# A two-layer attention and feed-forward prompt kernel: the first tiles taken one by one, and every engine's order written out

## The chip, the cores and the metric

The kernel runs on one core of a Trainium2 chip. A core has five engines with instruction streams of their own: TensorE (PE in the profile; PEld is its weight loads), VectorE (DVE), ScalarE (ACT), GpSimd (POOL) and SyncE (SP, which here only starts DMA transfers). An engine runs its own instructions strictly in the order in which they stand, and waits on semaphores for the others. The metric is the device time of the one launch in microseconds, as a median of several runs.

## The reference

The input x has 2048 tokens of 640 features. Two layers follow, each an attention with a memory over segments and then a feed-forward part, both with the same weights in both layers.

```python
    x = A_x
    x = x + _A_ref(_layernorm(x, axis=-1), A_wq, A_wk, A_wv, A_wo, A_beta)
    x = x + _B_ref(_layernorm(x, axis=-1), B_w1, B_w2)
    x = x + _A_ref(_layernorm(x, axis=-1), A_wq, A_wk, A_wv, A_wo, A_beta)
    x = x + _B_ref(_layernorm(x, axis=-1), B_w1, B_w2)
```

`_A_ref` splits the tokens into 4 segments of 512, with 32 heads of 20 features. In a segment it computes causal softmax attention within the segment, and a second term that is read from a memory matrix M and a normaliser z, which all earlier segments have written:

```python
            logits = jnp.einsum('bhqd,bhkd->bhqk', qs, ks) * scale + mask
            p = _softmax(logits, axis=-1)
            a_dot = jnp.einsum('bhqk,bhkd->bhqd', p, vs)
            pq = phi(qs)
            num = jnp.einsum('bhld,bhde->bhle', pq, M)
            den = jnp.einsum('bhld,bhd->bhl', pq, z)[..., None] + 1e-06
            o = g * (num / den) + (1.0 - g) * a_dot
            pk = phi(ks)
            M = M + jnp.einsum('bhld,bhle->bhde', pk, vs)
            z = z + jnp.einsum('bhld->bhd', pk)
```

(`a_mem` is written out here.) `_B_ref` is `maximum(x @ w1, 0) @ w2` with 1728 hidden features.

## The kernel before

Tokens are handled in tiles of 128, four of which make a segment. All of x and all weights stay in SBUF. Per layer and segment the work is: layer norm of the four tiles, with a transpose, so that features lie on partitions (`xnT`); the projections to q and k (`proj_part`, evacuated from PSUM into `stg`) and to v (`proj_v`, into `v_aug`); a way through device memory that spreads the heads of q and k over partitions (`spill` writes `scr`, `fill` reads it into `pad`; for the first two groups of heads `first_heads` copies straight from `stg`); scores of four heads at once as 20-row matmuls (`scores`, into the PSUM pairs X and Y); their exponentials on ScalarE (`exps`, into `PT`); the causal cut on GpSimd; values as 32-column matmuls (`apply`) or, for two early groups, by token (`values_by_token`); the memory's reading and writing (`mem_read`, `mem_write`); the output projection, and then the feed-forward part (`ffn`, `ffn_last`). Full-array matmul groups take one of four PSUM banks, the list `MISC`, and each bank is evacuated by VectorE or ScalarE before its next use.

Nothing of the order is written by hand. Each piece of work is a Python generator, called a stream, which yields operations with an engine, an estimated duration and the results that it waits for. `Sched` holds 33 streams with priorities and goes on picking the operation that can start first by its own clock. It places each on an engine (an evacuation may go to VectorE or ScalarE), gives out slots (PSUM banks, staging buffers), and puts semaphore waits in front. Where its clock shows TensorE idle for over 0.3 us, `keep_busy` puts in matmuls of a unit matrix that nobody reads (L638; dummies from here on). `plan` is run 48 times, each with another cost for changing between full-array, row-tiled and column-tiled matmuls (`STARTS`, 79 to 114 ns), and the plan with the least time in `late`, a replay with random lateness of the loads, is emitted.

The head is written apart. `first_ln_a` takes tiles 0 and 1 and `first_ln_b` tiles 2 and 3. Tiles 0, 1 and 3 have their statistics from VectorE (`stats`), tile 2 from ScalarE by two passes with accumulation. Both hand over to `first_pair`, which normalises two tiles on VectorE, transposes each on TensorE by the unit matrix (five 128-column matmuls) and copies the result from PSUM to `xnT`. `proj_first` then projects in groups of 256 columns, tiles 0 and 1 together, then tiles 2 and 3:

```python
        order = [(c, n, h) for h in range(2) for c in range(2) for n in range(2)]
        order += [(c, n, h) for c in range(2, FC) for h in range(2) for n in range(2)]
        for c, n, h in order:
            tk = yield from proj_part(0, 0, c, n, h)
```

Here c is the chunk of 128 output features, n is 0 for k and 1 for q, and h is the pair of tiles. From tile 0's arrival on, TensorE runs 43 dummies of `warm_pe` (L634).

Of the kernel before, what the change touches and what calls it, by code (L numbers as in the profile page):

```python
# [6 lines left out]
dt = mybir.dt  # L7
# [153 lines left out]
STARTS = [SWITCH_NS + 0.75 * (k - 48 // 2) for k in range(48)]  # L161
# [14 lines left out]

class Sched:


    def __init__(self, prog, switch):  # L180
        self.P = prog
        self.switch = switch
        self.log = []
        self.free = {e: 800.0 for e in ENGS}
# [8 lines left out]
    def keep_busy(self, op, start):  # L193
# [10 lines left out]
        if n > 1:  # L204
            self.log.append(("pe", 56.0 * n, 0.0, s.tks, [], False))
            self.P.waits("pe", s.tks)
            for _ in range(n):
                self.P.op("pe", lambda e, ap=s.ap: self.idle_fn(e, ap), False)
# [62 lines left out]
    def run(self):  # L271
        while True:
# [84 lines left out]
            self.log.append((e, hold, tail, waits, out if isinstance(out, list) else [out], op.dma is not None))  # L357
            st[2], st[3] = None, ((slot, out) if slot is not None else out,)

# [59 lines left out]
def plan(switch, sb, sem_, psum, dram, A_x, A_wq, A_wk, A_wv, A_wo, A_beta, B_x, B_w1, B_w2, out):  # L419
# [248 lines left out]
    def chain(t0, n, tk, sq=None):  # L668
# [7 lines left out]
        tk = yield pool(760, lambda e: e.tensor_tensor(rstd[:, sl], lnU[:, sl], mhalf[:, 0:n], ALU.pow), [tk] + h)  # L676
# [43 lines left out]
    def first_pair(p, tch):  # L720
        idt = yield Need("ident")
        if p == 0:
            xt = yield Acq(XNT_A)
            xt.users = []
            S.set("xts", 0, 0, tks=[xt])
        else:
            xt = yield Need("xts", 0, 0)
            xt = xt[0]
        bx = yield Acq(XN)
        done = []  # L730
        tns = []
        for k in range(2):
            tn = yield normed(2 * p + k, k, bx, tch[k])
            tns.append(tn)
        for k in range(2):
            t = 2 * p + k
            tn = tns[k]
            pb = lambda bk: bk.ap.bitcast(dt.bfloat16)
            fns = [(lambda e, bk, c=c, k=k: e.transpose(
                pb(bk)[:, c * 128:(c + 1) * 128], bx.ap[:, k * D + c * 128:k * D + c * 128 + 128], ident[:]),  # L740
                c == FC - 1) for c in range(FC)]
            bk, tT = yield pe((88.0 if p == 0 else 56.0) * FC, fns, [tn] + idt, acq=MISC)
            dst = xt.ap[:, t * FC:(t + 1) * FC, :].rearrange("p c n -> p (c n)")
            src = pb(bk)[:, 0:D]
            tc = yield evac(D, 1.5, lambda e, dst=dst, src=src: e.tensor_copy(dst, src),
# [783 lines left out]
def bass_interleave_layers__memory_aug_infini_attn__dense_activation_relu__prompt_kernel(  # L1529
    nc, A_x, A_wq, A_wk, A_wv, A_wo, A_beta, B_x, B_w1, B_w2, out,  # L1530
):
    with contextlib.ExitStack() as es:
# [13 lines left out]
        with nc.Block() as block:  # L1546
            S.P.emit(block)
# [29 lines left out]
```

## Time and profile before

| | us |
|---|---|
| median of 3 runs | 562.49 (562.12 to 563.04) |
| the profiled execution | 562.46 |
| its span in the trace | 560.6 |
| TensorE busy | 555.5 |
| VectorE busy | 410.8 |
| ScalarE busy | 409.7 |
| GpSimd busy | 194.3 |

A row of the timeline gives the start and the duration in microseconds, the engine, the line of the kernel, the operation and its tiles (written<-read), the shapes, and how many consecutive instructions were merged. In brackets stands how long the engine idled ahead of it, and what ended that. A matmul's duration contains its way through the array, during which the next ones already run; how densely they follow is seen from the distance of their starts. In the table of DMA issues the last number is the median time from issue to landing.

### The profile page before, as it was taken

How to read it: one execution, taken by the hardware profiler on the slowest of the kernel's cores; microseconds unless marked ns; L12 is line 12 of the kernel's file. 1: busy time of each engine (PE TensorE's matmuls, PEld its weight loads, DVE VectorE, ACT ScalarE, POOL GpSimd, SP SyncE). 2: the span in 40 equal slices, each digit the busy share in tenths (PEclk: the TensorE clock that was granted, in tenths of full speed). 3: DMA queues.
4: the chain of work that ended last, by engine and by line, in shares of the span. 5: the costliest groups of instructions: out<-in, count | busy, mean ns of one | idle time of the engine just before them, and what ended most of it. 6: DMA issues, size and time to landing. Idle time of an engine off the chain costs nothing.

```text
span 560.6 us, 12651 instructions
## 1 busy us (share of the span) xinstructions
PE 555.5 (99%) x5110; PEld 302.6 (54%) x5111; DVE 410.8 (73%) x1060; ACT 409.7 (73%) x522; POOL 194.3 (35%) x302
## 2 busy tenths in 40 slices
PE   8999999999999999999999999999999999999998
PEld 7654545545644455645356554465445654665655
DVE  5898899776998787877888987889824866651202
ACT  5799999987699779787897789877856788323140
POOL 4534344333354444344433443335401433100000
DMA  8599988741374137443373505550325510422101
GB/s 269 118 201 219 254 202 164 172 123 44 90 175 99 50 89 185 88 99 79 97 179 52 127 20 137 131 120 20 67 77 154 114 43 20 93 69 55 41 1 47
DMA packets 132219, 61.43 MB, mean 110 GB/s; under 512 B 111042, under 2 KB 122050, under 8 KB 132162
## 3 DMA queue, kind: packets, MB, share of 16 engines
q1 hardware_dynamic: 131942, 60.37, 45.7%
q8 instruction: 40, 0.66, 0.5%
q10 hardware_dynamic: 220, 0.26, 0.2%
q14 instruction: 17, 0.14, 0.1%
HBM read 20.57 MB, written 12.85 MB: 60 GB/s over the span
## 4 chain that ended last, share of the span: by engine, by line
PE 90%; DVE 8%; DMA 1%; ACT 0%; POOL 0%; issue 0%
PE ps L654 58%; PE ps L651 12%; PE ps L1114 9%; PE ps L1257 7%; DVE stats L662 2%; PE ps L1058 2%; PE ps L1007 2%; DVE x_sb L1328 1%; PE ps L1405 1%; DVE stg L827 1%; DMA x_sb<-in_A_x_dram 1%; DVE xn_tok L704 1%; DVE av L1265 0%; DVE xn_tok L716 0%; DVE mv L664 0%; ACT PT L1166 0%
## 5 line engine op out<-in xcount | busy, mean ns | idle before, releaser
L1166 ACT ACTIVATE PT<-ps 128x1024 bf16<-128x1024 f32 x320 | 310.1, 1022 | 66.1 <-PE ps L1114 64.5
L1178 POOL TENSOR_SCALAR_AFFINE_SELECT PT<-PT 128x512 bf16<-128x512 bf16 x256 | 166.3, 668 | 267.7 <-ACT PT L1166 267.7
L654 PE MATMUL ps<-w_r,hT 128*128 128x320 bf16 (+2 forms) x768 | 123.4, 299 | 0.1
L654 PE MATMUL ps<-xnT,w_r 128*128 128x512 bf16 x416 | 113.6, 379 | 0.0
L1328 DVE TENSOR_TENSOR x_sb<-x_sb,ps 128x320 bf16<-128x320 bf16 (+1 forms) x128 | 60.4, 479 | 70.2 <-PE ps L654 69.9
L654 PEld LDWEIGHTS ps<-w_r,hT 128*128 128x128 bf16 x768 | 72.2, 98 | 34.2 <-issue 6.3
L1436 ACT ACTIVATE hT<-ps 128x512 bf16<-128x512 f32 x55 | 33.0, 599 | 46.4 <-PE ps L654 46.1
L1114 PE MATMUL ps<-pad 20*128 20x384 bf16 (+3 forms) x1024 | 64.9, 301 | 0.0
L654 PEld LDWEIGHTS ps<-xnT,w_r 128*128 128x128 bf16 x416 | 39.7, 98 | 42.1 <-issue 2.9
L662 DVE BATCH_NORM_STATS2 stats<-x_sb 128x6 f32<-128x320 bf16 x126 | 55.9, 470 | 2.3 <-DMA x_sb<-in_A_x_dram 2.0
L1265 DVE CAST av<-ps 128x512 bf16<-128x512 f32 x56 | 38.3, 684 | 12.9 <-PE ps L1257 12.5
L1114 PEld LDWEIGHTS ps<-pad 20*128 20x128 bf16 x1024 | 18.2, 92 | 51.4 <-ACT PT L1166 24.2
L654 PE MATMUL ps<-wo_r,oT 128*128 128x320 bf16 x256 | 45.3, 299 | 0.0
L1434 DVE TENSOR_SCALAR hT<-ps 128x512 bf16<-128x512 f32 x49 | 33.5, 684 | 10.5 <-PE ps L654 10.0
L1257 PE MATMUL ps<-PT,v_aug 128*32 128x256 bf16 (+5 forms) x896 | 40.7, 302 | 0.0
L651 PE MATMUL ps<-xnT,w_r 128*128 128x512 bf16 x104 | 39.6, 381 | 0.0
L654 PE MATMUL ps<-wv_r,xnT 128*128 128x320 bf16 x192 | 35.8, 300 | 0.0
L654 PE MATMUL ps<-xnT,wk_r 128*128 128x512 bf16 (+1 forms) x140 | 35.5, 349 | 0.0
L676 POOL TENSOR_TENSOR rstd<-lnU,mhalf 128x2 f32<-128x2 f32 (+2 forms) x25 | 20.3, 811 | 39.9 <-DVE lnU L672 39.7
L654 PE MATMUL ps<-xnT,wq_r 128*128 128x512 bf16 (+1 forms) x140 | 33.9, 349 | 0.0
L1301 DVE TENSOR_TENSOR o_sb<-avt,rden 128x320 bf16<-128x320 bf16 x60 | 33.3, 572 | 0.7
L654 PEld LDWEIGHTS ps<-wo_r,oT 128*128 128x128 bf16 x256 | 24.8, 98 | 11.3 <-issue 1.3
(120 smaller groups left out, 686.9 us busy)
## 6 DMA issues: line engine op xcount, KB each, us to landing
pad<-scr SPq DMA_DIRECT2D x124, 80.0 KB
scr<-stg SPq DMA_DIRECT2D x34, 256.0 KB, 2.9
out_dram<-x_sb SPq DMA_DIRECT2D x15, 160.0 KB, 1.8
w_r<-in_B_w_dram SPq DMA_DIRECT2D x10, 216.0 KB, 3.3
w_r<-in_B_w_dram SPq DMA_DIRECT2D x13, 160.0 KB, 2.7
x_sb<-in_A_x_dram SPq DMA_DIRECT2D x9, 160.0 KB, 3.3
scr<-w_r SPq DMA_DIRECT2D x5, 256.0 KB, 3.5
x_sb<-in_A_x_dram SPq DMA_DIRECT2D x3, 320.0 KB, 7.3
```

Source lines behind the costliest of these rows:

```text
L651: bk, tk = yield pe(mm_ns(n), [(lambda e, bk, a=a, b=b: e.matmul(bk.ap[:, 0:n] if len(b.shape) == 2 else bk.ap[:, 0:n].rearrange("p (i n) ...
L654: tk = yield pe(mm_ns(n), [(lambda e, k=k, a=a, b=b, bk=bk: e.matmul(bk.ap[:, 0:n] if len(b.shape) == 2 else bk.ap[:, 0:n].rearrange("p (i ...
L662: tk = yield dve(320, 1, lambda e, c2=c2: e.bn_stats(stats6[:, t, c2, :], x_sb[:, t, c2 * 320:(c2 + 1) * 320]), xt)
L1114: fns.append([(lambda e, z=z, j=j, hh=hh, N=N, o=o, sl=sl: e.matmul(ps[:, hh, o:o + N], sl.ap[32 * hh:32 * hh + DH, z, 0, 128 * j:128 * j ...
L1166: tx = yield act(1024, lambda e, dst=dst, src=src: e.activation(dst, src, ACT.Exp, scale=SCALE), sc + pw)
L1178: tm = yield pool(600.0, lambda e, reg=reg: e.affine_select(out=reg, in_=reg, pattern=[[0, 4], [1, 128]], compare_op=ALU.is_ge, fill=0.0, ...
L1257: fns.append((lambda e, bk, j=j, hh=hh, pt=pt, g=g0 + z: e.matmul(bk.ap[32 * hh:32 * hh + wide(g, hh), 128 * j:L], VAUG[vx(a, s)][:, j].re ...
L1265: te = yield evac(L, 1, lambda e, sl=sl, z=z, bk=bk: e.tensor_copy(sl.ap[:, z], bk.ap), lambda e, sl=sl, z=z, bk=bk: e.activation(sl.ap[:, ...
L1301: to = yield dve(320, 1, lambda e, dst=dst, src=src, rz=rz: e.tensor_tensor(dst, src, rz, ALU.mult), [tg] + OSB.tks)
L1328: ta = yield dve(n, 1, lambda e: e.tensor_tensor(x_sb[:, t, c0:c0 + n], x_sb[:, t, c0:c0 + n], bk.ap[:, 0:n], ALU.add), [tk] + list(waits) ...
L1434: th = yield evac(512, 1, lambda e, dc=dc, bk=bk: e.tensor_scalar(hT[:, dc, :], bk.ap[:, :], 0.0, None, ALU.max), lambda e, dc=dc, bk=bk: ...
L1436: lambda e, dc=dc, bk=bk: e.activation(hT[:, dc, :], bk.ap[:, :], ACT.Relu), [tk] + HT.tks)
```

## The change

Three things change.

First, the head goes by single tiles. `first_tile(t)` replaces the two layer norm streams and `first_pair`. Tiles 0 and 1 have their statistics from VectorE, tiles 2 and 3 from ScalarE. Each tile has its own power on GpSimd, its own normalisation, transposes and copy. A list `TURN` fixes VectorE's order among them. The transposes go to the PSUM pairs X and Y in place of `MISC`. `proj_tile` projects tile 0 and tile 1 with 128-column matmuls, each into its half of the same bank, for the first two chunks of k and q, and one evacuation takes both halves. What then remains goes in groups of 256 as before, with the k group of chunk 2 on tiles 0 and 1 drawn ahead.

Second, one plan is made in place of 48, with a change of mode at 79 ns.

Third, the plan's order is not emitted. `Sched` records each operation with its stream, and `in_turns` lines them up anew: `TURNS` holds a string for each engine, in which each letter names the stream whose next operation comes (a is the first stream added, and so on; dummies stand as J on TensorE). Within a stream, on one engine, the order stays; which engine does an operation and which slot it has also stay as planned. Semaphore waits are derived again for the new order. The strings have 322 letters for SP, 518 for ScalarE, 1065 for VectorE, 299 for GpSimd and 2904 for TensorE, and were found by a search that moved runs of operations.

Counted in the built programs, TensorE has 5138 matmuls in place of 5111: 40 of 128 columns for 20 of 256, and 104 dummies for 97 (the 43 of `warm_pe` among them).

```diff
-STARTS = [SWITCH_NS + 0.75 * (k - 48 // 2) for k in range(48)]
+STARTS = [79.0]
...
+TURNS = {
+    "sp": (
+        "HHHHHHHHGHlllllmlmyyllllsmIIIIllslmeImlllIIIlIylysmIIIemmlIIIImlllllIIIsllmmlIIlgglyymeIlIlllmmjkels"
...
+    "pe": (
+        "FJJuzzzzzzvzzzzzzwzzzzzzzzzzzzzzzzzzxzzzzzzzzzzzzzzzzzzzzzzzzzzzzzCCzCCzzzzzzCCCCCCzzzzzCCCCCCCCCCCC"
...
+    def in_turns(self, turns):
...
+        for e, order in turns.items():
+            assert sorted(order) == sorted(n for n, rs in todo[e].items() for _ in rs), e
+            its = {n: iter(rs) for n, rs in todo[e].items()}
+            seq[e] = [next(its[n]) for n in order]
+        P = Prog(self.P.clk)
...
+                    P.waits(e, [new[t] for t in waits])
...
+    TURN = ["s0", "s0", "a0", "s1", "l0", "s1", "n0", "m2", "a1", "l1", "m3", "c0", "n1", "l2", "c1"]
...
+    def first_tile(t):
+        p, k = divmod(t, 2)
+        w = yield Need(("x0a", "x0b", "x01", "x01")[t])
+        if p == 0:
+            for c2 in range(2):
+                tk = yield from in_turn("s%d" % t, dve(320, 1.1, lambda e, c2=c2: e.bn_stats(
+                    stats6[:, t, c2, :], x_sb[:, t, c2 * 320:(c2 + 1) * 320]), w))
...
+        else:
+            junk = hT[:, 10 - 3 * k:13 - 3 * k, :].rearrange("p c n -> p (c n)")[:, 0:D]
+            ta = yield act(D + 350, lambda e: e.activation(
+                junk, x_sb[:, t, :], ACT.Copy, accum_out=asum[:, t:t + 1]), w, psum=False)
...
+        tch = yield pool(560, lambda e: e.tensor_tensor(
+            rstd[:, t:t + 1], lnU[:, t:t + 1], mhalf[:, 0:1], ALU.pow), [tk] + h)
...
+        bk, tT = yield pe((88.0 if t == 0 else 56.0) * FC, fns, [tn] + idt, acq=[X, Y])
...
+    def proj_tile(t, n, c):
...
+        for k in range(FC):
+            mm = lambda e, bk, k=k: e.matmul(
+                bk.ap[:, 128 * t:128 * t + 128], w_r[:, k, c * 128:(c + 1) * 128],
+                xt.ap[:, t * FC + k, :], start=(k == 0), stop=(k == FC - 1))
...
+        te = yield evac(256, 1, lambda e: e.tensor_copy(sg.ap[:, 0:256], src),
+                        lambda e: e.activation(sg.ap[:, 0:256], src, ACT.Copy), [tk] + sg.tks)
...
     def proj_first():
-        order = [(c, n, h) for h in range(2) for c in range(2) for n in range(2)]
-        order += [(c, n, h) for c in range(2, FC) for h in range(2) for n in range(2)]
+        for t in range(2):
+            for n in range(2):
+                for c in range(2):
+                    yield from proj_tile(t, n, c)
+        order = [(2, 0, 0)] + [(c, n, 1) for c in range(2) for n in range(2)]
+        order += [x for x in [(c, n, h) for c in range(2, FC) for h in range(2) for n in range(2)] if x != (2, 0, 0)]
...
-    S.add(5, first_ln_a())
-    S.add(5, first_ln_b())
+    for t in range(4):
+        S.add(1 + 0.2 * t, first_tile(t))
...
-            S.P.emit(block)
+            S.in_turns(TURNS).emit(block)
```

More of the change, by code (lines that the diff above doesn't have):

```diff
@@ L725, in first_pair @@
             S.set("xts", 0, 0, tks=[xt])
-        else:
[L727 to L745, printed above, removed]
-                            lambda e, dst=dst, src=src: e.activation(dst, src, ACT.Copy), [tT])
-            bk.release(tc)
-            done.append(tc)
```

202 lines of the change are left out of this document (169 added, 33 removed).

## The prediction

> **What bounds the kernel now.** I read the page first (engine shares, then the chain that ended last), then TensorE's timeline for the spacing of its matmuls and for its gaps, then the three engines at the head, then the DMA issues.
>
> ```profile
> PE 555.5 (99%) x5110; PEld 302.6 (54%) x5111; DVE 410.8 (73%) x1060; ACT 409.7 (73%) x522; POOL 194.3 (35%) x302
> ...
> PE 90%; DVE 8%; DMA 1%; ACT 0%; POOL 0%; issue 0%
> ```
>
> TensorE is busy for 99% of the span and carries 90% of the chain. A busy share counts pipelined matmuls whole, so the test is the distance from one start to the next.
>
> ```profile
> 30.63 0.38 PE L654 MATMUL ps<-hT,wk_r 128*128 128x512 bf16 x1
> 30.84 0.30 PE L651 MATMUL ps<-wv_r,hT 128*128 128x320 bf16 x1
> 30.98 0.71 PE L654 MATMUL ps<-wv_r,hT 128*128 128x320 bf16 x4
> 31.52 0.38 PE L654 MATMUL ps<-hT,wk_r 128*128 128x512 bf16 x1
> 31.83 0.39 PE L1114 MATMUL ps<-pad 20*128 20x512 bf16 x4
> 32.16 0.31 PE L651 MATMUL ps<-wv_r,hT 128*128 128x320 bf16 x1
> ...
> 557.39 0.83 PE L654 MATMUL ps<-w_r,hT 128*128 128x128 bf16 x12
> 558.06 0.22 PE L654 MATMUL ps<-w_u,hL 128*128 128x128 bf16 x1
> ```
>
> A start-to-start distance is 0.21 us for 512 columns (30.63 to 30.84), 0.135 for 320 (four in 30.98 to 31.52) and 0.056 for 128 (twelve in 0.67 us). The row at 31.52 is another 512-column matmul, but the score matmuls behind it start 0.31 us later: leaving full-array work for 20-row scores costs 0.096 us. The score block takes 0.33 us until the next full-array matmul. TensorE is bound by its own columns, so only three things can shorten the run: an earlier start of real work, fewer mode changes or dummies, and fewer gaps. The large gaps are these:
>
> ```profile
> 79.47 0.62 PE L638 MATMUL ps<-ident 128*128 128x128 bf16 x8
> 80.36 0.34 PE L1007 MATMUL ps<-BD,w_r 128*128 128x84 bf16 x3 [0.27 <-DVE om_sb L1018]
> ...
> 99.87 0.34 PE L1007 MATMUL ps<-BD,w_r 128*128 128x147 bf16 x3
> 100.47 0.31 PE L651 MATMUL ps<-wv_r,xnT 128*128 128x320 bf16 x1 [0.25 <-DVE av L1265]
> ...
> 324.17 0.38 PE L654 MATMUL ps<-xnT,w_r 128*128 128x512 bf16 x1
> 324.64 0.29 PE L638 MATMUL ps<-ident 128*128 128x128 bf16 x2
> ```
>
> Eight dummies fill 0.45 us after 79.47, and 80.36 leaves a gap of 0.44. The memory read at 99.87 holds three matmuls of some 0.06 us each, and 100.47 leaves 0.42. After 324.17, 0.47 less 0.21 is 0.26. Together that is 1.12 us in 550.
>
> **The head.**
>
> ```profile
> 4.86 0.74 ACT L764 ACTIVATE hT<-x_sb 128x640 bf16<-128x640 bf16 x1 [2.11 <-DMA x_sb<-in_A_x_dram]
> 5.50 0.19 ACT L764 ACTIVATION_READ_ACCUMULATOR hT<-x_sb 128x1 f32 x1
> 5.99 0.83 ACT L768 ACTIVATE hT<-x_sb,mv 128x640 bf16<-128x640 bf16 x1 [0.30 <-DVE mv L766]
> ...
> 6.87 0.43 DVE L716 TENSOR_SCALAR xn_tok<-x_sb,mv,rstd 128x640 bf16<-128x640 bf16 x1
> ...
> 7.88 0.48 DVE L745 COPY xnT<-ps 128x640 bf16<-128x640 bf16 x1
> ...
> 6.15 1.05 PE L638 MATMUL ps<-ident 128*128 128x128 bf16 x10
> 7.36 0.45 PE L739 MATMUL ps<-ident,xn_tok 128*128 128x128 bf16 x5 [0.15 <-DVE xn_tok L716]
> ...
> 9.06 0.81 PE L739 MATMUL ps<-ident,xn_tok 128*128 128x128 bf16 x10 [0.19 <-DVE xn_tok L716]
> 9.71 0.27 PE L651 MATMUL ps<-xnT,wk_r 128*128 128x256 bf16 x1
> ...
> 11.89 0.27 PE L651 MATMUL ps<-xnT,wk_r 128*128 128x256 bf16 x1
> ```
>
> Tile 0 stands transposed in SBUF at 8.36 (7.88 + 0.48), yet the first projection starts at 9.71, because it wants 256 columns, two tiles. The four groups on tiles 0 and 1 end at 11.89; call that point P.
>
> TensorE's head (transposes read xn_tok, projections wk_r and wq_r), before:
>
> ```order
> L634 MATMUL ps<-ident 128x128 x43
> L638 MATMUL ps<-ident 128x128 x10
> L739 MATMUL ps<-ident,xn_tok 128x128 x10
> L638 MATMUL ps<-ident 128x128 x5
> L739 MATMUL ps<-ident,xn_tok 128x128 x10
> L651 MATMUL ps<-xnT,wk_r 128x256
> L654 MATMUL ps<-xnT,wk_r 128x256 x4
> ```
>
> and after:
>
> ```order
> L742 MATMUL ps<-ident 128x128 x43
> L746 MATMUL ps<-ident 128x128 x9
> L893 MATMUL ps<-ident,xn_tok 128x128 x5
> L976 MATMUL ps<-xnT,wk_r 128x128 x6
> L893 MATMUL ps<-ident,xn_tok 128x128 x5
> L976 MATMUL ps<-xnT,wk_r 128x128 x4
> L976 MATMUL ps<-xnT,wq_r 128x128 x2
> L893 MATMUL ps<-ident,xn_tok 128x128 x5
> L976 MATMUL ps<-xnT,wq_r 128x128 x8
> L976 MATMUL ps<-xnT,wk_r 128x128 x10
> L893 MATMUL ps<-ident,xn_tok 128x128 x5
> L976 MATMUL ps<-xnT,wq_r 128x128 x10
> ```
>
> Projections of one tile now stand between the transposes, and six dummies are gone. What they wait for is on VectorE; before:
>
> ```order
> L662 BN_STATS stats<-x_sb 128x6
> L672 TENSOR_SCALAR lnU<-mv 128x1
> L662 BN_STATS stats<-x_sb 128x6
> L716 TENSOR_SCALAR xn_tok<-x_sb,mv,rstd 128x640
> L664 BN_AGGR mv<-stats 128x2
> L772 TENSOR_SCALAR lnU<-asum 128x1
> L774 TENSOR_SCALAR lnU<-mv 128x1
> L716 TENSOR_SCALAR xn_tok<-x_sb,mv,rstd 128x640
> L745 COPY xnT<-ps 128x640
> ```
>
> and after:
>
> ```order
> L853 BN_STATS stats<-x_sb 128x6
> L863 TENSOR_SCALAR mv<-asum 128x1
> L853 BN_STATS stats<-x_sb 128x6
> L824 TENSOR_SCALAR xn_tok<-x_sb,mv,rstd 128x640
> L855 BN_AGGR mv<-stats 128x2
> L863 TENSOR_SCALAR mv<-asum 128x1
> L857 TENSOR_SCALAR lnU<-mv 128x1
> L868 TENSOR_SCALAR lnU<-asum 128x1
> L900 COPY xnT<-ps 128x640
> ```
>
> Tile 0's copy moved ahead of the second normalisation, but behind tile 2's lnU (L868), which needs ScalarE's square.
>
> **The sum, part by part** (against the profiled execution, 562.46 us, which is 0.03 under the median of 562.49).
>
> A, the head. ScalarE now does two copies before the first square: 4.86 + 0.74, another 0.74, then 0.83 and its read of 0.19, about 7.4. So tile 2's lnU ends near 7.6, tile 0's copy near 8.15, and the first projection starts near 8.2. From there 40 matmuls and 15 transposes, 55 x 0.056 = 3.1 us, lead to P at about 11.35, against 11.89: -0.54. In columns the halves cost nothing: 40 x 0.056 = 2.24 against the 2.18 of 9.71 to 11.89. Bounds: -0.8 if lnU does not hold the copy back, 0 if the copies of tiles 1 to 3 come no earlier than now. The statistics of tile 3 move from VectorE to ScalarE and are in the 7.4. The load of beta moves ahead of the last x load on SP, and costs nothing there, since SP waits for keys at that point.
>
> B, mode changes. Counted in both orders, full-array work is left for scores or values 173 times before and 167 after: 6 x 0.096 = -0.58.
>
> C, dummies. Behind the head there stand 39 before (9, 8, 3, 6, 4, then 4, 2, 3) and 52 after (8, then 8, 9, 7, 8, 4, then 3, 5): 13 x 0.056 = +0.73. They are unconditional; where TensorE would wait anyway they are free, so the term's lower end is 0.
>
> D, gaps. Of the 1.12 us I let two thirds go, -0.75. The two near 80 and 100 us sit where the memory-read chain on VectorE is late, and the new order gives these places more dummies and leaves the reads later. I keep one third, because reuse distances shrink: the matmul work between an x addition's group and the next use of its bank is 1.9 us in the median, 2.2 before (lengths as above, laid over the order). Bounds: -1.12, and +2.0 (below).
>
> ScalarE and VectorE exchange some 2.5 us of evacuations. Both are at 73% and TensorE's work hides it; where that cover fails it shows in D. All other matmuls, and the tail from 544 us on, are the same.
>
> Sum: -0.54 - 0.58 + 0.73 - 0.75 = -1.14, so 561.3 us.
>
> The Trainium skill ("TensorE: Matmul & The Clock Gate", Back-to-back issue gap) speaks against part A: it puts a sustained stream of load and matmul at about 81 ns each for 128 columns. By it the 40 halves would take 3.24 us instead of 2.18, and the sum would be 562.3. The 0.056 us of the 557.39 row disagrees, and I go by the row.
>
> **The rivals.**
>
> Gaps only move. TensorE is bound by columns, so an order is worth little; the gaps of D stay at 1.12 or turn up elsewhere. For it: both orders contain the same columns. 562.46 - 0.54 - 0.58 + 0.73 = 562.1.
>
> Keys come late, the side that is slower. SP's order, fills of pad (the scores' operands) from the chip's memory (scr), before:
>
> ```order
> L945 DMA pad<-scr 20x2x1024 x4
> L900 DMA scr<-stg 128x1024
> L539 DMA x_sb<-in_A_x_dram 128x640 x3
> L900 DMA scr<-stg 128x1024
> L682 DMA_TRANSPOSE phk<-phs 128x12x128
> L945 DMA pad<-scr 20x2x1024 x8
> ```
>
> and after:
>
> ```order
> L1106 DMA pad<-scr 20x2x1024 x4
> L790 DMA_TRANSPOSE phk<-phs 128x12x128
> L1061 DMA scr<-stg 128x1024
> L647 DMA x_sb<-in_A_x_dram 128x640 x4
> L1106 DMA pad<-scr 20x2x1024 x2
> L790 DMA_TRANSPOSE phk<-phs 128x8x128
> L1106 DMA pad<-scr 20x2x1024
> L1061 DMA scr<-stg 128x1024
> L790 DMA_TRANSPOSE avt<-av 128x8x128
> L651 DMA wo_r<-in_A_wo_dram 128x640
> L1061 DMA scr<-w_r 128x1024
> L1106 DMA pad<-scr 20x2x1024 x3
> ```
>
> Eight fills that went out together are now cut up, and the fourth of a slot stands behind a spill (scr<-w_r) that waits for a VectorE evacuation.
>
> ```profile
> 33.71 3.62 SPq L945 DMA_DIRECT2D pad<-scr  x8
> ...
> scr<-w_r SPq DMA_DIRECT2D x5, 256.0 KB, 3.5
> ...
> avt<-av SPq DMA_TRANSPOSE x2, 4.9
> ```
>
> Laid over the order, 6.85 us of matmul work lie between the group that feeds that evacuation and the scores that use the slot. The evacuation (0.7), two issues (0.45 each, from 3.62 for eight) and a landing of 3.5 (scr row) need 5.1; a landing of 4.9 (avt row, between 20 and 60 us) needs 6.5, without any queue on VectorE. It decides once a landing or its queue is 1.7 us over the scr row. Four places stand under 7.3 us; at about 0.5 each TensorE loses 2.0, and 562.46 - 0.54 - 0.58 + 0.73 + 2.0 = 564.1.
>
> A cold array. The dummies run at about 0.10 us each (the 6.15 row), the matmuls from 7.36 on at half of that. Between tile 0's transposes and its projections some 0.8 us without dummies appear where now 0.4 is the most. If the array fell back, 55 matmuls would cost 55 x 0.05 = 2.75 more: 561.3 + 2.75 = 564.0. Against it: none of the gaps above slows what follows.
>
> **How the numbers follow.** I hold 0.2%, 1.12 us, as what can be told from no change. Forecast 0.52 (own range 560.4 to 562.1; 0.36 of it below 561.37, 0.16 above), gaps only move 0.18, keys late 0.20, cold array 0.04, the 81 ns rule 0.02, all gaps gone and the copy not held (562.46 - 0.8 - 0.58 + 0.73 - 1.12 = 560.7, with free dummies 560.0) 0.04. Faster: 0.36 + 0.04 = 0.40; same: 0.16 + 0.18 + 0.02 = 0.36; slower: 0.24. The range goes from 560.0, the last case, to 564.0: it cuts through the slower cases' middle and leaves out less than 0.2.
>
> **What would show it.** A: the first 128-column projection near 8.2 and P near 11.35. B: block lengths of 0.33 and exits of 0.096 unchanged. C: the dummies back to back with their neighbours, without gaps. D: no gap over 0.3 us after P. I am wrong if TensorE shows new gaps ahead of scores that wait for pad, if the projections at the head start 0.1 us apart, or if many gaps of some 0.1 us appear at bank reuses on VectorE.

## The result, and the profile after

The changed kernel takes 566.03 us (565.73 to 566.54, six runs) against 562.47 us (562.06 to 563.04, six runs): a ratio of 1.0063, 95% interval 1.0051 to 1.0076. It is slower by 3.6 us, where 1.2 us faster was forecast and 564.0 was the upper end of the range. The profiled execution takes 565.73 us, 3.27 more than the one profiled before; its span in the trace is 563.7.

Engine shares and the chain that ended last, from the page after:

```profile
PE 555.8 (99%) x5138; PEld 303.4 (54%) x5138; DVE 413.9 (73%) x1065; ACT 406.9 (72%) x519; POOL 193.3 (34%) x303
...
PE 82%; DVE 12%; DMA 2%; ACT 2%; POOL 1%; issue 0%; SPq 0%
```

The busy shares say nothing new. The chain does: TensorE carried 90% of it and now 82%, and VectorE has gone from 8% to 12%.

TensorE's timeline at the head, after:

```profile
7.19 0.45 PE L893 MATMUL ps<-ident,xn_tok 128*128 128x128 bf16 x5 [0.29 <-DVE xn_tok L824]
8.38 0.51 PE L976 MATMUL ps<-xnT,wk_r 128*128 128x128 bf16 x6 [0.73 <-DVE xnT L900]
8.73 0.45 PE L893 MATMUL ps<-ident,xn_tok 128*128 128x128 bf16 x5
...
11.47 0.27 PE L759 MATMUL ps<-xnT,wk_r 128*128 128x256 bf16 x1
```

The first projection of a single tile starts at 8.38 and point P (the four groups on tiles 0 and 1 done) is at 11.47, against 11.89: the head gains 0.42. Behind the long pause six matmuls take 0.35 us (8.38 to 8.73), 0.058 each.

TensorE's waits by what ended them, after (us in total, times, longest):

```profile
PE ps L976 <- DVE xnT L900: 0.7, 1, 0.7
PE ps L759 <- ACT PT L1327: 0.6, 1, 0.6
PE ps L759 <- DVE av L1426: 0.5, 2, 0.3
PE ps L759 <- DVE hT L1595: 0.4, 1, 0.4
PE ps L759 <- DMA hT<-xn_tok: 0.3, 1, 0.3
...
PE ps L1275 <- DMA pad<-scr: 0.3, 1, 0.3
PE ps L1168 <- DVE om_sb L1179: 0.2, 1, 0.2
```

The page of before had two such waits behind the head, 0.3 us each. To count everything, I call a gap what the distance between two starts on TensorE has over the first one's length (0.056, 0.135 or 0.216 us by its columns, with 0.096 more at a mode change and 0.33 for a score block), from 0.06 us on, later than 12 us. Before there are 8 of them, 1.64 us together; after there are 16, from 0.23 at 16.00 to 0.10 at 443.91, 5.0 us together. So 3.4 us of new gaps stand against 0.42 won at the head, 0.58 won at mode changes (167 are counted in the trace, 173 before) and 0.73 paid for dummies: 3.1 of the 3.27 us. Three of the new gaps, 0.23 at 16.00, 0.22 at 22.25 and 0.23 at 27.30, follow close on the head; the kernel before has none between 12 and 58. The first two wait for ScalarE, not VectorE.

Two of the new gaps, with VectorE's and GpSimd's rows beside TensorE's:

```profile
173.95 1.47 POOL L1339 TENSOR_SCALAR_AFFINE_SELECT PT<-PT 128x512 bf16<-128x512 bf16 x2 [2.06 <-ACT PT L1327]
...
174.15 1.62 DVE L1462 TENSOR_TENSOR o_sb<-avt,rden 128x320 bf16<-128x320 bf16 x2
...
175.69 2.47 DVE L1595 TENSOR_SCALAR hT<-ps 128x512 bf16<-128x512 f32 x4
...
177.02 0.39 PE L759 MATMUL ps<-xnT,w_r 128*128 128x512 bf16 x1 [0.41 <-DVE hT L1595]
...
182.82 1.47 POOL L1339 TENSOR_SCALAR_AFFINE_SELECT PT<-PT 128x512 bf16<-128x512 bf16 x2 [2.27 <-ACT PT L1327]
182.86 1.77 DVE L1462 TENSOR_TENSOR o_sb<-avt,rden 128x320 bf16<-128x320 bf16 x2
...
184.56 0.68 DVE L1426 CAST av<-ps 128x512 bf16<-128x512 f32 x1
...
185.29 0.31 PE L759 MATMUL ps<-wv_r,xnT 128*128 128x320 bf16 x1 [0.27 <-DVE av L1426]
```

In both, TensorE waits for an evacuation that stands behind two products o_sb<-avt,rden in VectorE's queue, and in both these take 0.8 to 0.9 us each while GpSimd does the causal cut (AFFINE_SELECT). Elsewhere they take 0.48. Laid over GpSimd's records, the 35 of them with hardly any GpSimd work beside them take 0.481 us in the mean, and the 11 wholly beside it 0.653. The addition x_sb<-x_sb,ps, with one operand in PSUM, takes 0.479 and 0.476. The Trainium skill ("SBUF — State Buffer", Who interferes with whom) says that a VectorE instruction with two inputs in SBUF contends with a GpSimd instruction that reads SBUF, and one with a single SBUF input outside the two-port modes doesn't; the trace agrees on which are held up. In the kernel before it is no different (33 at 0.479, 9 at 0.637); there fewer of the evacuations behind them held TensorE up (its gaps are 1.64 us).

### The profile page after: what moved, and what is told of

The parts are those of the page before. It is cut to its first block, busy times and chain, and to the rows that moved or that the text cites. A ratio compares the mean times of both kernels' runs of the same rounds, so it can differ in the third digit from the quotient of the medians.

```text
span 563.7 us, 12710 instructions
## 1 busy us (share of the span) xinstructions
PE 555.8 (99%) x5138; PEld 303.4 (54%) x5138; DVE 413.9 (73%) x1065; ACT 406.9 (72%) x519; POOL 193.3 (34%) x303
## 4 chain that ended last, share of the span: by engine, by line
PE 82%; DVE 12%; DMA 2%; ACT 2%; POOL 1%; issue 0%; SPq 0%
PE ps L762 54%; PE ps L759 11%; PE ps L1275 8%; PE ps L1418 6%; DVE stats L770 2%; PE ps L1168 1%; DVE xn_tok L812 1%; PE ps L1219 1%; DMA hT<-xn_tok 1%; DVE o_sb L1462 1%; DVE stg L958 1%; DVE hT L1595 1%; ACT PT L1327 1%; DMA pad<-scr 1%; DMA x_sb<-in_A_x_dram 1%; PE ps L1566 1%
## 5 line engine op out<-in xcount | busy, mean ns | idle before, releaser
L1275 PE MATMUL ps<-pad 20*128 20x512 bf16 (+3 forms) x1024 | 65.3, 301 | 0.4 <-DMA pad<-scr 0.3
L770 DVE BATCH_NORM_STATS2 stats<-x_sb 128x6 f32<-128x320 bf16 x120 | 53.5, 474 | 0.1
L1426 DVE CAST av<-ps 128x512 bf16<-128x512 f32 x54 | 36.9, 683 | 15.4 <-PE ps L1418 15.0
L762 PE MATMUL ps<-wo_r,oT 128*128 128x320 bf16 x256 | 46.8, 299 | 0.0
L1597 ACT ACTIVATE hT<-ps 128x512 bf16<-128x512 f32 x59 | 35.2, 601 | 16.0 <-PE ps L762 15.6
L1418 PE MATMUL ps<-PT,v_aug 128*32 128x128 bf16 (+4 forms) x896 | 40.7, 302 | 0.0
L784 POOL TENSOR_TENSOR rstd<-lnU,mhalf 128x2 f32<-128x2 f32 (+1 forms) x23 | 18.7, 814 | 57.9 <-DVE lnU L780 53.8
L958 DVE CAST stg<-ps 128x512 bf16<-128x512 f32 (+1 forms) x44 | 27.3, 631 | 10.9 <-PE ps L762 10.8
L1595 DVE TENSOR_SCALAR hT<-ps 128x512 bf16<-128x512 f32 x45 | 30.1, 679 | 6.5 <-PE ps L762 6.5
L1462 DVE TENSOR_TENSOR o_sb<-avt,rden 128x320 bf16<-128x320 bf16 x60 | 31.8, 552 | 0.3
```

Of the source, the lines that this page charges most:

```text
L762: tk = yield pe(mm_ns(n), [(lambda e, k=k, a=a, b=b, bk=bk: e.matmul(bk.ap[:, 0:n] if len(b.shape) == 2 else bk.ap[:, 0:n].rearrange("p (i ...
L770: tk = yield dve(320, 1, lambda e, c2=c2: e.bn_stats(stats6[:, t, c2, :], x_sb[:, t, c2 * 320:(c2 + 1) * 320]), xt)
L1275: fns.append([(lambda e, z=z, j=j, hh=hh, N=N, o=o, sl=sl: e.matmul(ps[:, hh, o:o + N], sl.ap[32 * hh:32 * hh + DH, z, 0, 128 * j:128 * j ...
L1418: fns.append((lambda e, bk, j=j, hh=hh, pt=pt, g=g0 + z: e.matmul(bk.ap[32 * hh:32 * hh + wide(g, hh), 128 * j:L], VAUG[vx(a, s)][:, j].re ...
L1426: te = yield evac(L, 1, lambda e, sl=sl, z=z, bk=bk: e.tensor_copy(sl.ap[:, z], bk.ap), lambda e, sl=sl, z=z, bk=bk: e.activation(sl.ap[:, ...
L1462: to = yield dve(320, 1, lambda e, dst=dst, src=src, rz=rz: e.tensor_tensor(dst, src, rz, ALU.mult), [tg] + OSB.tks)
```

## Experiments

Three theories, in the order in which they came up. One: the written turns used up the slack between TensorE and VectorE. Two: VectorE's operations from SBUF to SBUF are held up by GpSimd's cut, and the evacuations behind them come too late. Three: the kernel before holds a rare good order, and any change to the planner's input shuffles the rest and loses it. The rivals are the head with its buffers, and the order of transfers on SP. In each case "before" is the kernel before, run beside it: 562.6 to 562.8 us each time.

**The turns taken off, whole and in parts.** First the order of the planner alone:

```diff
-            S.in_turns(TURNS).emit(block)
+            S.P.emit(block)
```

> The new head and the new planner settings, but no written turns: every engine issues in the order in which the planner placed the work. Theory one (the written turns took the slack between TensorE and VectorE): the gaps of 5.0 us in the changed kernel's trace come from the turns and are gone here; 562.46 - 0.42 (the head as the changed kernel's trace shows it) + 0.7 at most (12 more dummies behind the head than before) = 562.0 to 562.8, with gaps of 1 to 2.5 us behind the head. Rival one (the head, its buffers or the planner settings are the cause): 565 to 566, with the gaps still there. Rival two (the order of DMA issues on SP): as theory one, since SP's turns are not used here either.

565.38 us (564.43 to 565.60), ratio 1.0045 (1.0031 to 1.0059). Theory one fell as it stood: 2.7 of the 3.6 us are there without any written turn. Its trace has P at 11.10, better than after, and gaps of 3.7 us behind 12 us, the same dummies (52) and as many mode changes as before (173).

Then parts of the table, the other engines in the planner's order:

```diff
-            S.in_turns(TURNS).emit(block)
+            S.in_turns({e: o for e, o in TURNS.items() if e in "sp dve pool".split()}).emit(block)
```

(second run: "sp dve pool pe"; third run: "dve pool pe").

> The written turns on SP, VectorE and GpSimd, while TensorE and ScalarE keep the planner's order. Theory one: VectorE's turns were made for another order of TensorE, so this is at best as good as the planner's own order and may be worse, 562.5 to 565; it says whether VectorE's turns alone bring the loss. Rival two (SP's turns: fills of pad cut up): 565 or more, with gaps ahead of score matmuls that wait for pad.

> All written turns but ScalarE's. Theory one: TensorE's and VectorE's turns are both there, so the loss is, too: 565 to 566.5, gaps of 4 to 6 us. If ScalarE's turns carried the loss (exps ahead of evacuations): 562.5 to 563.5.

> As the run without ScalarE's turns, and SP back in the planner's order as well. Theory one: within 0.5 of that run, 565 to 566.5. Rival two (SP's turns): 2 to 3 us less than that run, 562.5 to 563.5.

589.90 us (ratio 1.0485), 578.20 (1.0278) and 589.87 (1.0486). All three are 11.7 us and more above the ranges given; only the open "565 or more" of the first run's rival takes its number in, and that rival's sign, waits for pad, is 0.5 us there. TensorE then waits for evacuations and transfers everywhere (in the second run 2.8 us for stg from ScalarE and 2.3 for w_r from VectorE), and in the first and third the granted clock falls to 0.5 for 13.7 and 6.8 us in all. The table's strings fit only together, so these runs can't tell its parts apart, and they leave the rival open that SP's order brought the loss. What speaks against it comes later: with VectorE undisturbed the loss is gone although SP keeps its written order, and the changed kernel's trace has only one wait for pad, of 0.3 us.

**The cut made small.** One element of each row per cut instead of 512; the mask is not applied. The diff for the changed kernel; the planner's order and the kernel before have the same edit:

```diff
-                reg = PT[:, z, :, PT_OFF[j]:PT_OFF[j] + 128]
+                reg = PT[:, z, 0:1, PT_OFF[j]:PT_OFF[j] + 1]
...
-                    out=reg, in_=reg, pattern=[[0, 4], [1, 128]], compare_op=ALU.is_ge, fill=0.0, base=0,
+                    out=reg, in_=reg, pattern=[[0, 1], [1, 1]], compare_op=ALU.is_ge, fill=0.0, base=0,
```

> The changed kernel with GpSimd's causal cut reduced to one element per call (work left out: the mask is not applied, so the output is not the reference's); all orders and waits stay. Theory two (VectorE's operations from SBUF to SBUF take some 0.65 us instead of 0.48 while GpSimd cuts, and the evacuations queued behind them come too late for TensorE): the gaps behind the head fall from 5.0 us to 2.5 or less, 562.5 to 563.5. Rival (the order alone: the waits would be there at unstretched durations, too): 565.3 to 566.

> The planner's order of the changed kernel, without the written turns, with the same reduced cut (mask not applied). Theory two: 565.4 less 2 or so of its 3.7 us of gaps, 562.5 to 563.8. Rival: 564.8 to 565.5.

> The kernel before with the same reduced cut (mask not applied). Both theories: its gaps behind the head are 1.6 us, so it can gain 1.6 at most: theory two 561.2 to 562.2, rival 562.2 to 562.6. The distance to the changed kernel's run of this kind is what the order costs when VectorE is not disturbed: 1 to 2 by theory two, 3 to 3.5 by the rival.

562.08 us for the changed kernel (ratio to before 0.9990, 0.9980 to 0.9999), 563.61 for the planner's order (1.0014, 1.0004 to 1.0024), 561.46 for the kernel before (0.9979, 0.9970 to 0.9988). The three gain 4.0, 1.8 and 1.1 us, in the direction of theory two (the first ends 0.4 below its range), and the distance between changed kernel and kernel before shrinks from 3.6 to 0.6. For the planner's order it shrinks only from 2.7 to 2.2, so most of what that order loses is not GpSimd's doing. Undisturbed, the written turns are 1.5 us better than the planner's order; with the real cut they are 0.8 worse, so they are the order that the hold-up hurts most. VectorE's busy time falls from 413.9 to 394.5 us, and by as much in the kernel before (410.8 to 392.1). But this also lets the values' matmuls have their operand earlier, by the 0.45 us that a cut is shorter.

**A cut that is long again, in two ways.** First one element for the readers, then a cut of 224 elements on a spare tile (spare_cut) for which nobody waits:

```diff
+                rest = lambda e: e.affine_select(
+                    out=spare_cut[:], in_=ident[:, None, 0:112].to_broadcast([128, 2, 112]), pattern=[[0, 2], [1, 112]],
+                    compare_op=ALU.is_ge, fill=0.0, base=0, channel_multiplier=-1)
+                tm, RESTS["last"] = yield Op([("pool", 600.0, [(one, True), (rest, True)], 60.0)], ex + [RESTS["last"]])
```

> The changed kernel with each causal cut split in two on GpSimd: one element of the scores' block first, which releases the readers (mask not applied, as in the run with the reduced cut), then a cut of 224 elements on a spare tile that nobody waits for. GpSimd is busy beside VectorE again, but the values' matmuls get their operand as early as in the run with the reduced cut. If VectorE's stretched operations cause the loss: its operations from SBUF to SBUF are long again, gaps 4 us or more, 564.5 to 566.5. If instead the shorter way from exp over cut to values brought the gain: 562 to 563.

561.97 us (0.9994, 0.9985 to 1.0003), which looks like the second case but settles nothing. The spare cuts take 0.41 us each and VectorE's busy time only goes back to 400.1, 5.6 of the 19.4 us. So the other way round: hold the readers back without disturbing VectorE. A power operation on one column, and then the cut of one element; no two-input operation of VectorE beside a power operation had been seen to be longer than elsewhere, though the run with the reduced cut has only one product phs<-phs,rtmp beside one (0.413 us, the others 0.418). The run itself, below, bears it out: 27 products o_sb<-avt,rden that meet a power operation take 0.484 us in the mean, the 33 others 0.482.

```diff
+                hold = lambda e: e.tensor_tensor(spare_cut[:, 0:1], spare_cut[:, 1:2], spare_cut[:, 1:2], ALU.pow)
+                HOLDS["last"], tm = yield Op([("pool", 600.0, [(hold, True), (one, True)], 60.0)], ex + [HOLDS["last"]])
```

> The changed kernel with each causal cut replaced by a power operation on one column of a spare tile and then a cut of one element, which releases the readers (mask not applied). GpSimd holds the readers back for about 0.8 us, longer than the cut's 0.67, but in the run with the reduced cut no VectorE operation beside a power operation was longer than elsewhere. If VectorE's stretched operations cause the loss: 562 to 563, as with the reduced cut. If the shorter way from exp over cut to values brought that run's gain: 565.5 to 567.

> The kernel before with the same replacement (mask not applied). If VectorE's stretched operations are the cause: 561 to 562, as with the reduced cut. If the way over the cut is: 562.5 to 563.5.

561.92 us for the changed kernel (0.9988, 0.9978 to 0.9998) and 561.84 for the kernel before (0.9984, 0.9975 to 0.9994). GpSimd's groups and VectorE's product in the changed kernel with the slow cut, and then that product in the changed kernel itself:

```profile
L1346 POOL TENSOR_TENSOR spare_cut<-spare_cut 128x1 f32<-128x1 f32 x256 | 149.9, 586 | 224.1 <-ACT PT L1329 223.5
...
L1343 POOL TENSOR_SCALAR_AFFINE_SELECT PT<-PT 128x1 bf16<-128x1 bf16 x256 | 54.9, 215 | 0.0
...
L1469 DVE TENSOR_TENSOR o_sb<-avt,rden 128x320 bf16<-128x320 bf16 x60 | 27.6, 483 | 0.3
```

```profile
L1462 DVE TENSOR_TENSOR o_sb<-avt,rden 128x320 bf16<-128x320 bf16 x60 | 31.8, 552 | 0.3
```

GpSimd is busy for longer than with the real cut (216.9 us, 193.3 before the edit) and holds the readers for 0.80 us instead of 0.67, and still the loss is gone. What matters is that VectorE's operations are not held up. By the rule above, TensorE's gaps in this trace are 1.7 us, against 5.0 in the changed kernel, and 1.2 in the kernel before with the slow cut; the three between 16 and 28 stay (0.73 us). ScalarE's exponentials take the same 1.02 us in all of them. The place that had the first gap above, in this run (timeline of GpSimd, VectorE, TensorE):

```profile
172.10 0.90 POOL L1346 TENSOR_TENSOR spare_cut<-spare_cut 128x1 f32<-128x1 f32 x1 [2.02 <-ACT PT L1329]
172.11 0.88 DVE L1469 TENSOR_TENSOR o_sb<-avt,rden 128x320 bf16<-128x320 bf16 x2
...
172.91 1.87 DVE L1602 TENSOR_SCALAR hT<-ps 128x512 bf16<-128x512 f32 x3
...
173.86 1.03 PE L764 MATMUL ps<-xnT,w_r 128*128 128x512 bf16 x4
...
174.72 0.38 PE L761 MATMUL ps<-xnT,w_r 128*128 128x512 bf16 x1
```

The two products take 0.88 us together instead of 1.62, the evacuation follows at 172.91, and TensorE goes on without a gap. Without the hold-up the two orders are 0.1 us apart here and 0.6 with the reduced cut, where they were 3.6 apart.

**The planner's input.** One number of the diff in the kernel before, whose 48 plans come down to the one at 79:

```diff
-STARTS = [SWITCH_NS + 0.75 * (k - 48 // 2) for k in range(48)]
+STARTS = [79.0]
...
-        tk = yield pool(760, lambda e: e.tensor_tensor(rstd[:, sl], lnU[:, sl], mhalf[:, 0:n], ALU.pow), [tk] + h)
+        tk = yield pool(600, lambda e: e.tensor_tensor(rstd[:, sl], lnU[:, sl], mhalf[:, 0:n], ALU.pow), [tk] + h)
```

> The kernel before with one number of the change: the planner's cost of the power operation on GpSimd is 600 instead of 760, and the planner setting that the kernel before ends up with (79) is kept. Head and everything else as before. Theory three (the kernel before holds a rare good order, and any change to the planner's input shuffles the rest of the order and loses it): 564 to 567 with new gaps of 2 to 4 us. Rival (the new head with its buffers is what costs): 562.2 to 563.

574.81 us (1.0228, 1.0202 to 1.0255): 12 us, far over what was expected. Some of TensorE's waits in it:

```profile
PE ps L1007 <- DVE om_sb L1018: 3.0, 4, 1.9
...
PE ps L739 <- DVE xn_tok L716: 1.1, 1, 1.1
PE ps L1058 <- DMA phk<-phs: 0.9, 1, 0.9
PE ps L1257 <- POOL PT L1178: 0.6, 1, 0.6
```

One duration that is off by 0.16 us in the planner's eyes shuffles the order of the whole kernel. But the run takes away more than that: it keeps the plan at 79, where the kernel's own way is to choose the best of 48. The planner's own replay (`late` in the kernel's code, the mean of its four) gives the kernel before's plan 563.0 us, this one 571.3, and the best of the 48 plans with the same number, the one at 91, 565.3. By that account the greater part of the 12 us is the missing choice, and some 2 us are the number; no run on the chip separates them. For the changed kernel the replay gives 565.0, and 79 would be the choice of its 48, too. So the planner's order at 565.38 needs no fault in the new head to be worse than the one before; theory three holds in that sense, for 2 us or so.

**The old order behind the new head.** The planner is made to take, step by step, the choices that it took for the kernel before, with the new head's operations free (core of the edit; the operations of the head follow the planner):

```diff
-            for prio, n, st, alts, op, late in heads:
+            n0, k0, l0 = self.order[self.step] if self.step < len(self.order) else (None, 0, False)
+            heads = [(p, n, st, al if n in free else [x for x in al if x[2] == k0], op, late)
+                     for p, n, st, al, op, late in heads
+                     if n in free or n == n0 and getattr(op, "lone", False) == l0]
+            for prio, n, st, alts, op, late in heads:
...
-            S.in_turns(TURNS).emit(block)
+            S.P.emit(block)
```

In the traces, the last 5018 of TensorE's 5125 weight loads have the names and shapes of the kernel before in the same order, save for a few that start at the same moment; on VectorE it is the last 993 of 1060, on ScalarE 491 of 524, on GpSimd 292 of 303.

> The new head (planner's order of it) with the kernel before's order behind it: the planner is made to choose step by step what it chose for the kernel before, and no written turns. Theory three (the head is a gain, and the loss is in the shuffled order behind it): P near 11.1 as in the planner's own order of the changed kernel, 0.8 earlier than before, gaps behind the head 1.6 as before, 562.5 - 0.8 = 561.7 (561.2 to 562.2). Rival (the head's buffers in PSUM or its pace cost later on): 562.5 to 564.

> The new head with the kernel before's order behind it, with the cut reduced to one element per call (mask not applied). With the cut this order lost 2.4 us to the kernel before though both issue the same work in the same order behind the head. If the loss is that VectorE's operations meet GpSimd's cuts at other moments: 561 to 562, within 0.5 of the kernel before with the reduced cut (561.46). If it lies in the head's buffers or in late transfers: 563.5 or more.

565.04 us (1.0043, 1.0031 to 1.0056) and, with the reduced cut, 562.97 (1.0008, 0.9998 to 1.0018). The first is above both of its cases, the second between them. The same work in the same order is 2.4 us slower behind the new head. Instruction by instruction against the kernel before, it leads by 0.57 us at P, by 0.30 at the first matmul with wv_r (13.77) and by nothing at 14.76, where the row names VectorE's evacuation of a projection:

```profile
14.76 0.28 PE L763 MATMUL ps<-xnT,wk_r 128*128 128x256 bf16 x1 [0.15 <-DVE stg L962]
```

The wait for wv_r is plain in the profiled execution of the changed kernel with the reduced cut, at 563.07 us the slowest of its ten; there the load landed 9.2 us after its issue, against 8.0 in the changed kernel and 8.8 in the kernel before:

```profile
13.91 0.30 PE L759 MATMUL ps<-wv_r,xnT 128*128 128x320 bf16 x1 [0.74 <-DMA wv_r<-in_A_wv_dram]
```

Then the run with the old order falls back by 0.3 near 32, 0.2 near 84, 0.9 between 93 and 99, 0.7 at 284 and 0.3 at 336. A place on the way, near 86: GpSimd and VectorE in the timeline of the kernel before, and then of this one:

```profile
85.58 1.46 POOL L1178 TENSOR_SCALAR_AFFINE_SELECT PT<-PT 128x512 bf16<-128x512 bf16 x2 [1.88 <-ACT PT L1166]
...
86.13 0.42 DVE L975 TENSOR_TENSOR phs<-phs,rtmp 128x512 bf16<-128x512 bf16 x1
```

```profile
85.84 1.22 POOL L1343 TENSOR_SCALAR_AFFINE_SELECT PT<-PT 128x512 bf16<-128x512 bf16 x2 [1.88 <-ACT PT L1331]
...
86.58 0.76 DVE L1140 TENSOR_TENSOR phs<-phs,rtmp 128x512 bf16<-128x512 bf16 x1
```

The cut comes 0.26 later and the product 0.45 later, and the product takes 0.76 us instead of 0.42: whether a product is held up depends on the moment at which it meets the cut. But the reduced cut takes away only 0.9 of the 2.4 us (2.38 apart with the cut, 562.97 - 561.46 = 1.51 without). Laid against the kernel before with the reduced cut, that run's trace shows where they are: it leads by 0.68 us at P, loses 0.60 of it at 14.63 to an evacuation by VectorE (stg), wins 0.20 near 58, and loses 0.94 near 83 to a transpose of o_sb that comes late, 0.25 at 282 to one of phs, and 0.34 near 334; in these two executions it ends 1.2 us behind. Why the transposes come late stays open, and with it the rival that the head or its buffers cost something behind it in this order.

**The dummies.** Those behind the head left out, in the changed kernel and in the run with the old order:

```diff
+                    if seq[e][at[e]][1] == len(self.streams) and at[e] > 20:
+                        fns, waits = [], []
```

> The changed kernel without its 52 dummy matmuls behind the head (those in the head stay). They are 52 x 0.056 = 2.9 us of TensorE. If they cost what the prediction's term C charges, every one: 563.1. If most stand where TensorE would wait anyway: 565 to 566. If TensorE runs slower behind a pause: 566.5 or more.

> As the run with the new head and the old order, without the 39 dummies behind the head: 39 x 0.056 = 2.2 us at most. If half stand where TensorE waits anyway: 1.1 less than that run, 560.6; if all do, no change; if TensorE runs slower behind a pause, above that run.

566.97 us (1.0080, 1.0066 to 1.0094), 0.9 over the changed kernel, and 565.38 (1.0052, 1.0038 to 1.0065), 0.3 over the run with the dummies, which is within the spread of the runs. Busy time by stretches of 2 us in the first of these (columns: stretch, sum, then PE, PEld, DVE, ACT, POOL, the granted clock, the DMA share and GB/s):

```profile
80.00:82.00 2.00, 1.17 (x11) 0.37 (x11) 2.00 (x6) 2.00 (x3) 2.00 (x4) 1.00 0.48 110
82.00:84.00 2.00, 1.61 (x27) 0.61 (x26) 1.97 (x5) 2.00 (x3) 1.68 (x3) 1.00 1.02 226
84.00:86.00 2.00, 1.41 (x8) 0.54 (x9) 1.90 (x7) 1.52 (x3) 0.87 (x3) 0.62 0.85 176
86.00:88.00 2.00, 2.00 (x11) 1.29 (x10) 0.81 (x3) 2.00 (x3) 0.89 (x2) 0.53 0.97 94
```

TensorE is busy for 1.17 us of 2, and some microseconds later the granted clock is at 0.62 and 0.53; a 320-column matmul then takes 0.27 us instead of 0.135. The clock is at 0.5 from 84.5 us on for 3.4 us, and in the second of these runs from 81.3 on for as long; in the changed kernel, with its dummies near 80 us, it stays at 1.00. So the dummies don't cost what term C charged: taking them away saved nothing in either run, and cost 0.9 us in the first.

**VectorE's turns edited.** With the cut as it is, at eight places of the VectorE string an evacuation, or the product that a memory read waits for, goes ahead of an operation between SBUF operands, for example (f is the normalising of values, whose two letters here are o_sb<-avt,rden; d the values' evacuation; D the feed-forward part, here hT's evacuation):

```diff
-        "fdffDDDDpCqnqffqCAffdqqCqnAodoq...
+        "fdfDDfDDpCqnqffqCAfdfqqCqnAodoq...
```

> The changed kernel with eight places of VectorE's written order edited: at each, an evacuation or a read's result that TensorE waited for in the trace now stands ahead of one operation from SBUF to SBUF that GpSimd's cut had held up (and behind which it stood). The eight gaps are 0.31 + 0.38 + 0.31 + 0.57 + 0.44 + 0.69 + 0.30 + 0.27 = 3.3 us. If VectorE's queue ahead of these evacuations is what TensorE waits for, half to all of it goes: 562.8 to 564.5. If the waits have another cause (the slots' readers elsewhere, ScalarE, transfers) or only move: 565.2 to 566.5.

> As the run with eight edited places, but the one near 250 us is left as in the changed kernel: there the edit put a sum of outputs behind two evacuations, and the transpose that reads it came 2.7 us late and let TensorE's clock fall. Seven gaps, 2.6 us: 563.0 to 564.0 if VectorE's queue is the cause, without runs near 568. If the edits only moved the waits: 565 to 566.5.

The eight edits give 564.32 us (1.0043, 1.0024 to 1.0062), within what was expected, the seven 564.25 (1.0029, 1.0017 to 1.0040; 563.01 to 564.95). With eight, all eight gaps are gone (one of 0.26 near 104 is new), but the edit near 250 us put the sum o_sb<-o_sb,om_sb behind two evacuations, the transpose that reads it came late, and TensorE stood still and was then granted half its clock:

```profile
255.59 0.45 PE L759 MATMUL ps<-wo_r,oT 128*128 128x320 bf16 x1 [2.70 <-DMA oT<-o_sb]
```

```profile
256.00:258.00 2.00, 2.00 (x21) 0.61 (x22) 0.49 (x1) 0.32 (x1) 0.00 (x0) 0.50 0.04 8
```

(first a row of TensorE's timeline of that run, then one of its busy time by stretches, with the granted clock of 0.50 behind the engines). Three of its nine runs, the profiled one among them, are at 567.5 to 568.2 with a mean granted clock of 0.994 to 0.997, where the other six have 1.0. With the seven, TensorE's waits are, whole:

```profile
PE ps L742 <- POOL mhalf L695: 1.6, 1, 1.6
PE ps L759 <- ACT PT L1327: 0.6, 1, 0.6
PE ps L976 <- DVE xnT L900: 0.6, 1, 0.6
PE ps L759 <- DMA hT<-xn_tok: 0.3, 1, 0.3
PE ps L1275 <- ACT PT L1327: 0.2, 1, 0.2
```

No row behind the head names VectorE any more. The 0.6 us put down to ScalarE are the place near 250 that was left as it was: the matmul at 249.47, whose weight load waits for VectorE's hT; and a gap of 0.26 near 104, which this table leaves out, waits for VectorE's av. The ratio to the kernel before goes from 1.0063 to 1.0029, about half of the loss; the profiled execution, at 563.01, is the fastest of the seven, and its gaps are 2.5 us. The expected 563.0 to 564.0 was missed by 0.25. No version here beats the kernel before.

## Why the prediction was wrong

**A, the head, -0.54.** Right in kind, too large: -0.42 in the profile. The reason given for the copy's lateness held (it starts at 7.84, behind tile 2's lnU), the first projection came at 8.38 instead of 8.2. What the prediction didn't ask is whether the lead can be kept: the run with the old order shows 0.57 us of lead used up at 14.76, half of it at the first matmul that needs wv_r, half at an evacuation of a projection. In the changed kernel the three gaps between 16 and 28, 0.68 us together, are more than the lead of 0.42; whether they are its price was not tested.

**B, mode changes, -0.58.** The counts (173 and 167) and the block lengths stand (score blocks 0.33, exits 0.096 in the trace after). No run isolates the term; with the slow cut the two orders differ by 0.1 us, where -0.42 - 0.58 + 0.73 would be -0.27, so nothing speaks against it by more than the runs can tell.

**C, dummies, +0.73.** "Unconditional", and so a cost of 0.056 each: the runs without them were slower by 0.9 us and, within the spread, by 0.3. The lower end given, 0, was not low enough, since a row of dummies can also keep the clock.

**D, gaps, -0.75.** This is the step that failed, in sign. "Of the 1.12 us I let two thirds go": the gaps went from 1.64 us (the three that were shown and five of about 0.1) to 5.0, +3.4. Of the three large ones only that at 324 is gone; 0.54 stand between 83 and 85 in three pieces in place of the one at 80, and 0.38 near 100. The reasoning was that late chains at two places get more dummies; of VectorE it said that at 73% "TensorE's work hides it". That cover is what failed. The working took VectorE's durations as fixed, while 60 products of one shape had a mean of 0.572 on the page of before,

```profile
L1301 DVE TENSOR_TENSOR o_sb<-avt,rden 128x320 bf16<-128x320 bf16 x60 | 33.3, 572 | 0.7
```

where 33 that stood alone took 0.479. The shorter reuse distances were noted (1.9 us instead of 2.2), and "many gaps of some 0.1 us at bank reuses on VectorE" was named as what would prove it wrong; they came fewer and larger, 0.3 to 0.7 each. And the upper bound of D, +2.0, was taken from the keys alone. Only the runs without disturbing cuts name the cause: 3.0 (reduced cut) and 3.5 (slow cut) of the 3.6 us between the two kernels go with them, and seven gaps with the moved evacuations. Even undisturbed, the gaps did not shrink as forecast: 1.7 us against the kernel before's 1.2.

**The rivals.** "Gaps only move" was nearer than the forecast, but they grew. "Keys come late" had the side right and the mechanism wrong: of its four places one shows, and it costs 0.33 us, not 2.0:

```profile
336.90 0.39 PE L1275 MATMUL ps<-pad 20*128 20x512 bf16 x4 [0.27 <-DMA pad<-scr]
```

The cold array did not come at the head: the 0.73 us without work there are followed by matmuls of 0.058. A fall of the granted clock came in the two runs without dummies, in the run with eight edits and in two of the runs with parts of the table. The 81 ns rule is refuted by the same row: 40 halves and 15 transposes take 3.09 us from 8.38 to 11.47, 0.056 each. (Part A's own figures, 8.2 and 3.1, give 11.3 for P and not the 11.35 that its term goes by.)

**What was not asked at all** is where the new order comes from. The written turns were moved from an order that the planner had made for another head and another duration, and that order alone is 2.7 us slower than the old one, 2.2 of them with VectorE undisturbed. The turns save it six mode changes, and with VectorE undisturbed 1.5 of those 2.2 us; with the real cut they end 0.8 us above it (3.56 against 2.74, each to the kernel before run beside it).

## What to carry to other kernels

An order written out, or planned, with fixed durations is good only as long as the durations are: before costing such a change, look in the profile for groups of one shape whose mean lies over their shortest, find what stands beside the long ones, and count the evacuations queued behind them. Where a planner makes the order, a number in its input that looks harmless can be worth more than the edit, so run the planner's own order apart from what is built upon it. And a lead won at the head is only a lead if the next transfer has landed and the next buffer is free by then.

## What the runs showed of the hardware that I had not expected

Wholly beside GpSimd's work, which is nearly always the cut (0.67 us), VectorE's products o_sb<-avt,rden take 0.65 us in the mean and 0.94 at most instead of 0.48. They are not alone: the normalisations xn_tok<-x_sb,mv,rstd, which read one tile and two values per token, take 0.553 us in the mean and 0.437 with the reduced cut, and are the largest part of the 19 us that VectorE's 414 lose with it. A power operation of GpSimd on one column (0.59 us), reading SBUF too, does not lengthen the products. The Trainium skill ("SBUF — State Buffer", Who interferes with whom) makes no such difference between GpSimd's operations that read SBUF, and no run here shows what it is. At 13.66 us an operation of VectorE that takes 0.28 us in most places (rtmp<-stg) took 1.16 beside two memsets of GpSimd.

The granted clock fell to 0.5 in a standstill of 2.7 us, and again, in the run without dummies, after a stretch in which TensorE was busy for 60 to 80% without a single wait as long as 1 us. The Trainium skill ("TensorE: Matmul & The Clock Gate", Why this matters for your kernels) asks for no pauses over about 3 us; here less was enough, and it cost half the speed for 6.8 and 3.4 us.
